# A gated spectral and feed-forward mix: first block loaded in halves, last gated part moved, last store in halves

## The chip, the cores and the metric

The kernel runs on one core of one Trainium2 chip. The metric is device time in microseconds (us): the median of three runs before the change is 1020.85 us (1020.79 to 1021.39). The engines are TensorE (PE, with its weight loads as PEld), VectorE (DVE), ScalarE (ACT), GpSimd (POOL) and SyncE (SP); SP, ACT and POOL each have a queue on which they issue DMAs.

## The reference

```python
x = A_x                                        # 1 x 2048 x 640, fp32
g = sigmoid((x * gate_w).sum(-1))
a = x @ dft_hid_re.T ;  b = x @ dft_hid_im.T
fnet = dft_seq_re @ a - dft_seq_im @ b         # 2048 x 2048 by 2048 x 640
ffn = (gelu(x @ w_gate) * (x @ w_up)) @ w_down # hidden size 1728
return g * fnet + (1 - g) * ffn
```

All in fp32. The kernel gets that precision by splitting an operand into a high part (a copy rounded to the fp32r type) and a low part (the rest), and forms each product from three fp32r matmuls: high by high, high by low, low by high.

## The kernel before, in words

Everything is tiled to 128 partitions, and the 2048 rows of x lie in four column blocks of 512, taken as two pairs. The program has stages: the hidden layer of the feed-forward part (first its plain 128 columns and a mixed remainder, then the rest in a scheme of sums that saves products), the product with w_down, the sequence transform (which makes u), and the last product of u with the hidden-size transform, whose results are multiplied by the gate and added to what already lies in the output.

**The start.** Inside `in_order(ACT, DVE, PE, SP)`, which fixes the order on each engine to that of the code, line 1072 issues the first weights on ACT's queue and line 1073 the first block of x, 128 partitions by 512 columns, on SP's; then SP issues four more weight pieces and four more x pieces. `first_parts` (line 1052) makes the parts of a piece: ACT the high part of x (line 1055), DVE the first weights' high part (line 1057), then DVE the low part of x (line 1060) and of the weights (line 1061). `first_block` (line 379) runs on TensorE, for each of the five pieces, three matmuls high by high (line 387) into three accumulators (pm, pg, pu), three with the low part of x (line 389) and three with the low weights (line 391). Seven matmuls on zeros stand ahead of it.

**The end.** The last of four groups in the u stage needs five parts of u, numbered 15 to 19 in the tile names. TensorE runs `tail` over them for X, Z and V (lines 1552 and 1563), for L (lines 1570, 1571, one accumulator of 512 columns and one of 256), and last 30 matmuls of 256 columns into `last` (yLast, line 1578), which work on gated parts of u. `gated_u` (line 1332) makes one: two products with the gate on DVE (ug, line 1337), the high part on ACT and the low part on DVE (both ue, line 1339). Its calls stand between the sums of Z and V (line 1564), the last one behind them (line 1568). Each sum of Z or V is a DVE instruction that adds the accumulator (line 1566), then `give` (line 1460): a product with the gate on DVE and a store of 256 KB on POOL's queue that adds to the output. ACT and DVE are in the order of the code here too. The end of the program is three plain stores: the first L block by POOL, the second by SP (line 1575), and the 256 columns of `last`, copied by DVE and stored by SP (lines 1580, 1581).

Names: x011h and x011l are the high and low part of the first x pieces, w0h and w0l of the weights, xr and w0r the raw loads; yx and ys are the results of V and Z, yl those of L and `last`.

Of the kernel before, what the change touches and what calls it, by code (L numbers as in the profile page):

```python
# [8 lines left out]
F32 = mybir.dt.float32  # L9
F32R = mybir.dt.float32r  # L10
BF16 = mybir.dt.bfloat16
AF = mybir.ActivationFunctionType
ALU = mybir.AluOpType

P = 128
S, D, F = 2048, 640, 1728
T = 512
NT = S // T
ND = D // P
# [11 lines left out]
def kernel(  # L31
# [27 lines left out]
    nc = tc.nc  # L59
# [11 lines left out]
    def mtile(dt, name):  # L71
        return pool.tile([P, T], dt, tag="m", name=name, bufs=12)
# [4 lines left out]
    def high(hi, raw):  # L77
        nc.scalar.activation(hi, raw, AF.Copy)  # L78
# [300 lines left out]
    def first_block(W, B, tp, t, parts, then):  # L379

        ps = [bank(f"p{n}{tp}{t}") for n in "mgu"]
        ws = [W[n] for n in "mgu"]
        for d in range(ND):
            rh, rl = xpart(B, d, t)
            parts(d)
            for p, w in zip(ps, ws):
                nc.tensor.matmul(p, w[d][0], rh, start=d == 0, stop=False, skip_group_check=True)
            for p, w in zip(ps, ws):
                nc.tensor.matmul(p, w[d][0], rl, start=False, stop=False, skip_group_check=True)
            for p, w in zip(ps, ws):  # L390
                nc.tensor.matmul(p, w[d][1], rh, start=False, stop=d == ND - 1, skip_group_check=True)
        pm, pg, pu = ps
        then()
        mixed_out(pm, tp, t)
        ge = mtile(F32, f"ge{tp}{t}")
        nc.scalar.activation(ge, pg, AF.Gelu_apprx_tanh)
        tt(ge, ge, pu, op=ALU.mult)
        keep(h0[tp], t - 1, ge)
# [643 lines left out]
    B, tiles, load, piece, tsum, his, lows = load_x(0)  # L1042

    def load_piece(d, t):
        raw, src, _ = piece(d, t)
        nc.sync.dma_start(raw, src)
# [5 lines left out]
    def first_parts(d):  # L1052
        raw, _, (xh, xl) = piece(d, 1)
        wh, wl, wr = parts0(d)
        high(xh, raw)
        if d == 0:
            nc.vector.tensor_copy(wh, wr)
        else:
            high(wh, wr)
        low(xh, xl, raw)  # L1060
        low(wh, wl, wr)
# [8 lines left out]
    with in_order(ACT, DVE, PE, mybir.EngineType.SP):  # L1070
        tiles(1)
        load0(nc.scalar, 0)
        load_piece(0, 1)
        for d in range(1, ND):
            load0(nc.sync, d)
            load_piece(d, 1)
        tiles(2)
        load(2)
        pw = bank("pwarm")
        for _ in range(7):  # L1080
            nc.tensor.matmul(pw, warm[:, :P], warm, start=True, stop=True, skip_group_check=True)
        first_block(W0, B, 0, 1, first_parts, second_parts)
        B0, (tsum0, his0, lows0) = B, (tsum, his, lows)
        Bs.append(B)
        B, tiles, load, piece, tsum, his, lows = load_x(1)
        tiles(1)
        load(1)
        tiles(2)
        load(2)
        mixed(Wm, B0, 0, 2)  # L1090
        his((1, 1), (2, 1))
        lows((1, 1), (2, 1))
        split_piece(4, 1)
        plain_gate_up(W0, B0, 0, 2)
        tsum0(1)
        tsum0(3)
        mixed(Wm, B, 1, 1)
        his((1, 2), (2, 2))
        his0("T1", "T3")
        lows((1, 2), (2, 2))  # L1100
        split_piece(4, 2)
        lows0("T1")
        tsum0(2)
        lows0("T3")
        his0("T2")
        tsum0(4)
        plain_gate_up(W0, B, 1, 1)
        his0("T4")
        lows0("T2", "T4")
        W = load_w(1)  # L1110
        nc.sync.dma_start(gwb, gw.to_broadcast([P, D]))
        tsum(1)
        tsum(3)
        mixed(Wm, B, 1, 2)
        his("T1", "T3")
        lows("T1")
        tsum(2)
        lows("T3")
        his("T2")
        tsum(4)  # L1120
        his("T4")
        lows("T2", "T4")
        plain_gate_up(W0, B, 1, 2)
# [50 lines left out]
    p, f = 1, 3  # L1174
# [112 lines left out]
    H = T // 2  # L1287
# [44 lines left out]
    def gated_u(i):  # L1332

        r = ugs[i]
        v = slot(F32, [P, 2, H], f"ug{i}")
        for q in range(2):
            tt(v[:, q], r[q][:, 1, H:], gw[1][:, 1, H:], op=ALU.mult)
        e = slot(F32R, [P, 2, 2, H], f"ue{i}")
        split(e[:, 0], e[:, 1], v)
        ugs[i] = [(e[:, 0, q], e[:, 1, q]) for q in range(2)]  # L1340
# [128 lines left out]
    for i, (tp, b, p) in enumerate(useq[: 3 * ND]):  # L1469
# [22 lines left out]
        if not b:  # L1492
            for q in range(2):
                sv["c11", q] = copy(X[q], f"ys{n}{q}")
            for q in range(2):
                c = sv["c11", q]
# [64 lines left out]
    for k, (ps, w, b, t) in enumerate(((Z, "S4", 3, 1), (V, "A12", 2, 0))):  # L1561
        for q in range(2):
            tail(ps[q], (w, q, True), b)
            gated_u(3 * ND + 2 * k + q)
            v = es[q][t]
            tt(v, v, ps[q], op=ALU.add)
            give(1, 2 * q, t, v)
    gated_u(3 * ND + 4)
    for t, cols, ps in ((0, slice(0, T), L[0]), (1, slice(0, H), L[1][:, :H])):
        tail(ps, ("e5", 0, True), t, cols)  # L1570
        tail(ps, ("e5", 1, False), 2 + t, cols)
# [4 lines left out]
    for q in range(2):  # L1576
        for p in range(ND):
            mm3(last, ukw[0, p]["e5"][q], ugs[3 * ND + p][q], False, p == ND - 1)
    v = mtile(F32, "yl2")[:, :H]
    nc.vector.tensor_copy(v, last)  # L1580
    nc.sync.dma_start(out[3, 4, :, H:], v)
    order.close()


# [62 lines left out]
```

## Time and profile before

| | us |
|---|---|
| median of 3 runs | 1020.85 |
| profiled execution, its own time | 1020.78 |
| its span | 1019.0 |
| TensorE busy | 1013.6 (99%) |
| VectorE busy | 811.6 (80%) |
| ScalarE busy | 494.9 (49%) |
| GpSimd busy | 145.5 (14%) |

The span runs from the first to the last thing the profiler saw; 1.78 us of the execution's own time lie outside it. Times in rows count from the span's start. A matmul's busy time overlaps the next one's, since matmuls are pipelined: the start-to-start distance tells the pace.

### The profile page before, as it was taken

What the parts mean: (1) busy time and instruction counts of PE and PEld (TensorE: products, weight loads), DVE (VectorE), ACT (ScalarE), POOL (GpSimd) and SP (SyncE); (2) the same over time, 40 slices, a digit from 0 to 9 for tenths busy, and PEclk for the clock granted to TensorE, in tenths of its full rate; (3) what the DMA queues carried; (4) which work ended last, traced back from release to release, by engine and by line L of the source; (5) the groups of instructions that cost most, each with busy time, mean ns of one, the idle gap of its engine ahead of it and who ended that gap; (6) DMA issues with size and microseconds to landing.
All of it is one profiled execution on the core that took longest, in us unless ns stands there. A gap on an engine that the chain in (4) does not pass through costs nothing.

```text
span 1019.0 us, 13152 instructions
## 1 busy us (share of the span) xinstructions
PE 1013.6 (99%) x4488; PEld 835.3 (82%) x4488; DVE 811.6 (80%) x1148; ACT 494.9 (49%) x660; POOL 145.5 (14%) x259
## 2 busy tenths in 40 slices
PE   9999999999999999999999999999999999999998
PEld 7888888888888888887888888888888888888887
DVE  6988887978778939967898976878687769797777
ACT  5455455545365637456455443434443345455431
POOL 0113130212123100100010022002100200021013
PEclk9999999999999999999999999999999999999999
DMA  8358797959699978877866579657965878697748
GB/s 283 138 189 300 267 331 235 350 198 351 208 344 365 359 257 275 294 245 259 294 222 219 198 265 333 237 199 264 336 210 195 303 245 289 249 388 219 258 97 132
DMA packets 87795, 265.01 MB, mean 260 GB/s; under 512 B 11216, under 2 KB 19440, under 8 KB 87728
## 3 DMA queue, kind: packets, MB, share of 16 engines
q1 hardware_dynamic: 65392, 194.47, 56.0%
q0 software_dynamic: 22192, 69.50, 20.1%
q8 instruction: 35, 0.57, 0.2%
q14 instruction: 32, 0.26, 0.1%
q10 hardware_dynamic: 144, 0.20, 0.1%
HBM read 194.38 MB, written 69.75 MB: 259 GB/s over the span
## 4 chain that ended last, share of the span: by engine, by line
PE 87%; issue 8%; DVE 2%; POOL 1%; DMA 1%; ACT 1%; POOLq 0%; ACTq 0%; DVEq 0%
PE pX L89 4%; PE pX L90 4%; PE pX L91 4%; PE pL L89 3%; PE pL L90 3%; PE pL L91 3%; PE px L89 3%; PE px L91 3%; PE px L90 3%; PE pZ L89 2%; PE pZ L90 2%; PE pZ L91 2%; PE pV L89 2%; PE pV L90 2%; PE pV L91 2%
## 5 line engine op out<-in xcount | busy, mean ns | idle before, releaser
L78 ACT ACTIVATE ch<-csa 128x1024 fp32r<-128x1024 f32 x32 | 34.0, 1063 | 75.2 <-DVE csa L868 66.9
L81 DVE TENSOR_TENSOR cl<-cra,ch 128x1024 fp32r<-128x1024 f32 x32 | 39.2, 1224 | 28.8 <-ACT ch L78 23.4
L78 ACT ACTIVATE ch<-cra 128x1024 fp32r<-128x1024 f32 x32 | 33.9, 1060 | 57.0 <-PE pY L90 19.2
L81 DVE TENSOR_TENSOR cl<-crb,ch 128x1024 fp32r<-128x1024 f32 x32 | 39.1, 1223 | 13.5 <-ACT ch L78 11.4
L90 PE MATMUL pL<-cl,xah 128*128 128x512 f32 x128 | 49.8, 389 | 0.0
L91 PE MATMUL pL<-ch,xal 128*128 128x512 f32 x128 | 49.8, 389 | 0.0
L89 PE MATMUL pL<-ch,xah 128*128 128x512 f32 x128 | 49.3, 389 | 0.0
L78 ACT ACTIVATE ch<-crb 128x1024 fp32r<-128x1024 f32 x32 | 33.8, 1057 | 22.6 <-DVE cl L81 7.8
L81 DVE TENSOR_TENSOR cl<-csb,ch 128x1024 fp32r<-128x1024 f32 x32 | 39.2, 1225 | 2.0 <-ACT ch L78 0.5
L81 DVE TENSOR_TENSOR cl<-csa,ch 128x1024 fp32r<-128x1024 f32 x32 | 39.1, 1221 | 1.7 <-PE pL L90 0.7
L78 ACT ACTIVATE ch<-csb 128x1024 fp32r<-128x1024 f32 x32 | 34.0, 1064 | 10.3 <-DVE csb L871 6.4
L350 POOL DMA_DIRECT2D hA<-s x48 | 26.2, 546 | 83.1 <-DVE s L708 52.2
L707 ACT ACTIVATE s<-s 128x512 f32<-128x512 f32 x20 | 12.7, 633 | 49.1 <-DVE s L548 33.0
L81 DVE TENSOR_TENSOR kl<-kw,kh 128x1024 fp32r<-128x1024 f32 (+1 forms) x26 | 31.5, 1211 | 3.6 <-ACT kh L78 3.6
L78 ACT ACTIVATE kh<-kw 128x1024 fp32r<-128x1024 f32 (+1 forms) x26 | 27.2, 1046 | 7.9 <-DVE kw L926 4.7
L981 POOL DMA_DIRECT2D out<-ks x12 | 6.5, 543 | 167.1 <-DVE ks L980 166.5
L548 DVE TENSOR_TENSOR s<-s,px 128x512 f32<-128x512 f32 x12 | 8.2, 686 | 27.5 <-ACT s L630 25.9
L1343 POOL DMA_DIRECT2D uA<-c x8 | 4.3, 543 | 170.9 <-DVE c L1430 170.7
L350 POOL DMA_DIRECT2D hT<-s x48 | 26.0, 543 | 17.9 <-DMA hA<-s 3.1
L91 PEld LDWEIGHTS pL<-ch,xal 128*128 128x128 f32 x128 | 24.0, 188 | 5.0
L89 PEld LDWEIGHTS pL<-ch,xah 128*128 128x128 f32 x128 | 24.0, 188 | 5.0
L90 PEld LDWEIGHTS pL<-cl,xah 128*128 128x128 f32 x128 | 24.0, 188 | 5.0
(3089 smaller groups left out, 3471.4 us busy)
## 6 DMA issues: line engine op xcount, KB each, us to landing
cra<-in_ct SPq DMA_DIRECT2D x64, 512.0 KB, 4.0
crb<-in_ct SPq DMA_DIRECT2D x64, 512.0 KB, 4.8
xx<-xtd SPq DMA_DIRECT2D x42, 512.0 KB, 6.1
hA<-s POOLq DMA_DIRECT2D x48, 256.0 KB, 5.9
hT<-s POOLq DMA_DIRECT2D x48, 256.0 KB, 6.4
kr<-hA SPq DMA_DIRECT2D x24, 512.0 KB, 7.9
kr<-hT SPq DMA_DIRECT2D x24, 512.0 KB, 6.3
ux<-uA SPq DMA_DIRECT2D x24, 512.0 KB, 6.0
```

Source lines behind the costliest of these rows:

```text
L78: nc.scalar.activation(hi, raw, AF.Copy)
L81: nc.vector.tensor_tensor(lo, raw, hi.bitcast(F32), op=ALU.subtract)
L89: nc.tensor.matmul(ps, lh, rh, start=first, stop=False, skip_group_check=True)
L90: nc.tensor.matmul(ps, lh, rl, start=False, stop=False, skip_group_check=True)
L91: nc.tensor.matmul(ps, ll, rh, start=False, stop=last, skip_group_check=True)
L350: nc.gpsimd.dma_start(to[:, i], src)
L548: tt(a, a, c, op=ALU.add)
L707: nc.scalar.activation(s2, s2, AF.Gelu_apprx_tanh)
L981: nc.gpsimd.dma_start(out[2 * tp + t, e], src)
L1343: nc.gpsimd.dma_start(to[:, i], src)
```

## The change

Three places are edited. The first x block is loaded as two column halves, the left on SP's queue and the right on ACT's behind the weights; its high part is made in two halves and the first three matmuls become six of 256 columns. The last gated part (19) is made between the sums of the two V halves instead of behind both. The last copy and store is cut in two: 128 columns by DVE and SP, 128 by ACT and its queue.

```diff
@@ first_block
-            for p, w in zip(ps, ws):
-                nc.tensor.matmul(p, w[d][0], rh, start=d == 0, stop=False, skip_group_check=True)
+            for c in (slice(0, T // 2), slice(T // 2, T)) if d == 0 else (slice(0, T),):
+                for p, w in zip(ps, ws):
+                    nc.tensor.matmul(p[:, c], w[d][0], rh[:, c], start=d == 0 and c.start == 0, stop=False, skip_group_check=True)
@@ first_parts
-        high(xh, raw)
         if d == 0:
+            for c in (slice(0, T // 2), slice(T // 2, T)):
+                high(xh[:, c], raw[:, c])
             nc.vector.tensor_copy(wh, wr)
         else:
+            high(xh, raw)
             high(wh, wr)
@@ loads
         load0(nc.scalar, 0)
-        load_piece(0, 1)
+        raw, src, _ = piece(0, 1)
+        for queue, c in ((nc.sync, slice(0, T // 2)), (nc.scalar, slice(T // 2, T))):
+            queue.dma_start(raw[:, c], src[:, c])
@@ the end
             tail(ps[q], (w, q, True), b)
             gated_u(3 * ND + 2 * k + q)
+            if k and not q:
+                gated_u(3 * ND + 4)
             v = es[q][t]
             tt(v, v, ps[q], op=ALU.add)
             give(1, 2 * q, t, v)
-    gated_u(3 * ND + 4)
...
-    v = mtile(F32, "yl2")[:, :H]
-    nc.vector.tensor_copy(v, last)
-    nc.sync.dma_start(out[3, 4, :, H:], v)
+    for name, c in (("yl2", slice(0, P)), ("yl3", slice(P, H))):
+        v = mtile(F32, name)[:, c]
+        if c.start:
+            nc.scalar.activation(v, last[:, c], AF.Copy)
+        else:
+            nc.vector.tensor_copy(v, last[:, c])
+        (nc.scalar if c.start else nc.sync).dma_start(out[3, 4, :, H + c.start : H + c.stop], v)
```

The order of instructions at the places that the prediction speaks of. A semaphore in brackets is one that the instruction waits for: DMAHW of a DMA issued by SP or ACT, DMASW of one issued by POOL.

ACT at the start of the program, before (w0r and xr are the raw weights and x):

```order
L200 DMA w0r0_141<-in_w0 128x384
L78 ACT_TABLE_LOAD
L78 ACTIVATE x011h_151<-xr011_150 128x512 [waits DMAHW1_49]
L78 ACTIVATE x011h_151<-xr011_150 128x512 [waits DMAHW3_49]
L78 ACTIVATE w0h0_144<-w0r0_141 128x384 [waits DMAHW2_49]
```

ACT at the same place, after:

```order
L200 DMA w0r0_141<-in_w0 128x384
L1078 DMA xr011_150<-in_xt 128x256
L78 ACT_TABLE_LOAD
L78 ACTIVATE x011h_151<-xr011_150 128x256 [waits DMAHW1_49]
L78 ACTIVATE x011h_151<-xr011_150 128x256 [waits DMAHW3_49]
L78 ACTIVATE x011h_151<-xr011_150 128x512 [waits DMAHW4_49]
L78 ACTIVATE w0h0_144<-w0r0_141 128x384 [waits DMAHW2_49]
```

ACT issues a second DMA behind the weights, and the first high part is two instructions, each with a wait of its own.

DVE near the end, before: the gated parts 17, 18 and 19 (ug, ue), the V sums (yx0, yx1) and the first L sum:

```order
L81 TENSOR_TENSOR ue17_8590<-ug17_8587,ue17_8590 128x512
L1566 TENSOR_TENSOR yx0_8489<-yx0_8489,yVlast0_8470 128x512
L1461 TENSOR_TENSOR yx0_8489<-yx0_8489,gw1_7708 128x512
L1337 TENSOR_TENSOR ug18_8611<-ux180_8315,gw1_7708 128x256
L1337 TENSOR_TENSOR ug18_8611<-ux181_8316,gw1_7708 128x256
L81 TENSOR_TENSOR ue18_8614<-ug18_8611,ue18_8614 128x512
L1566 TENSOR_TENSOR yx1_8513<-yx1_8513,yVlast1_8471 128x512
L1461 TENSOR_TENSOR yx1_8513<-yx1_8513,gw1_7708 128x512
L1337 TENSOR_TENSOR ug19_8620<-ux190_8359,gw1_7708 128x256
L1337 TENSOR_TENSOR ug19_8620<-ux191_8360,gw1_7708 128x256
L81 TENSOR_TENSOR ue19_8623<-ug19_8620,ue19_8623 128x512
L1573 TENSOR_TENSOR yl0_8656<-yLlast0_8472,gw1_7708 128x512
```

DVE at the same place, after:

```order
L81 TENSOR_TENSOR ue17_8595<-ug17_8592,ue17_8595 128x512
L1342 TENSOR_TENSOR ug19_8598<-ux190_8364,gw1_7713 128x256
L1342 TENSOR_TENSOR ug19_8598<-ux191_8365,gw1_7713 128x256
L81 TENSOR_TENSOR ue19_8601<-ug19_8598,ue19_8601 128x512
L1573 TENSOR_TENSOR yx0_8494<-yx0_8494,yVlast0_8475 128x512
L1466 TENSOR_TENSOR yx0_8494<-yx0_8494,gw1_7713 128x512
L1342 TENSOR_TENSOR ug18_8622<-ux180_8320,gw1_7713 128x256
L1342 TENSOR_TENSOR ug18_8622<-ux181_8321,gw1_7713 128x256
L81 TENSOR_TENSOR ue18_8625<-ug18_8622,ue18_8625 128x512
L1573 TENSOR_TENSOR yx1_8518<-yx1_8518,yVlast1_8476 128x512
L1466 TENSOR_TENSOR yx1_8518<-yx1_8518,gw1_7713 128x512
L1579 TENSOR_TENSOR yl0_8661<-yLlast0_8477,gw1_7713 128x512
```

Part 19 stands ahead of both V sums now, part 18 between them as before, and the second V sum right ahead of L.

ACT at the very end, after (before, nothing followed the last ue):

```order
L78 ACTIVATE ue17_8595<-ug17_8592 128x512 [waits DVE_49,Activation_49]
L78 ACTIVATE ue19_8601<-ug19_8598 128x512 [waits DVE_49,Activation_49]
L78 ACTIVATE ue18_8625<-ug18_8622 128x512 [waits DVE_49]
L1588 ACTIVATE yl3_8732<-yLast_8527 128x128 [waits DMASW3_49,DMASW1_49,DVE_49]
L1591 DMA out_0<-yl3_8732 128x128 [waits Activation_49]
```

ACT's copy of the last 128 columns and its store are new.

## Rows read from the trace of the kernel before

**Rows 1.** Waits of TensorE: line, releaser: total us, times, longest.

```profile
...
PE pm L387 <- ACT x011h L78: 0.5, 1, 0.5
PE yLast L90 <- DVE ue L81: 0.3, 1, 0.3
```

**Rows 2.** Timeline of the start: start, length (us), engine, line, op, tiles [idle before].

```profile
...
0.74 0.41 ACTq L200 DMA_DIRECT2D w0r<-in_w  x1
...
4.12 0.63 ACT L78 ACTIVATE x011h<-xr 128x512 fp32r<-128x512 f32 x1 [1.66 <-DMA xr<-in_xt]
...
4.33 0.36 DVE L1057 CAST w0h<-w0r 128x384 fp32r<-128x384 f32 x1 [3.19 <-DMA w0r<-in_w]
...
4.83 0.63 PE L387 MATMUL pm<-x011h,w0h 128*128 128x512 f32 x1 [0.47 <-ACT x011h L78]
...
5.76 0.39 PE L389 MATMUL pm<-x011l,w0h 128*128 128x512 f32 x1
...
```

**Rows 3.** Timeline of the last 15 us, the same columns.

```profile
...
1005.80 0.69 DVE L81 TENSOR_TENSOR ue<-ug,ue 128x512 fp32r<-128x512 f32 x1 [0.76 <-ACT ue L78]
...
1006.41 0.68 DVE L1566 TENSOR_TENSOR yx<-yx,yVlast 128x512 f32<-128x512 f32 x1
...
1007.13 0.69 DVE L1461 TENSOR_TENSOR yx<-yx,gw 128x512 f32<-128x512 f32 x1
...
1007.74 0.75 DVE L1337 TENSOR_TENSOR ug<-ux,gw 128x256 f32<-128x256 f32 x2
...
1008.59 0.63 ACT L78 ACTIVATE ue<-ug 128x512 fp32r<-128x512 f32 x1 [2.81 <-DVE ug L1337]
...
1009.25 0.69 DVE L81 TENSOR_TENSOR ue<-ug,ue 128x512 fp32r<-128x512 f32 x1 [0.76 <-ACT ue L78]
...
1011.01 0.28 PE L89 MATMUL yLast<-ue,uw00h 128*128 128x256 f32 x1
...
1011.67 0.88 POOL L1462 DMA_DIRECT2D out<-yx  x1 [2.58 <-DVE yx L1461]
...
1012.33 0.28 PE L91 MATMUL yLast<-ue,uw03l 128*128 128x256 f32 x1
...
1013.24 0.68 DVE L1573 TENSOR_TENSOR yl<-yLlast,gw 128x512 f32<-128x512 f32 x1
...
1015.02 0.43 DVE L1574 TENSOR_TENSOR yl<-yl,av 128x256 f32<-128x256 f32 x1
...
1015.71 0.42 DVE L1580 COPY yl<-yLast 128x256 f32<-128x256 f32 x1 [0.26 <-PE yLast L91]
1016.16 0.34 SPq L1581 DMA_DIRECT2D out<-yl  x1
```

**Rows 4.** Stretches: us, busy by engine, granted clock, DMA share, GB/s.

```profile
...
1.75:3.00 1.25, 1.25 (x5) 0.42 (x3) 0.00 (x0) 0.71 (x1) 0.00 (x0) 1.00 0.74 213
3.00:4.70 1.70, 1.36 (x4) 0.18 (x2) 0.36 (x1) 0.58 (x1) 0.00 (x0) 1.00 1.05 391
1013.00:1014.80 1.80, 1.46 (x13) 1.42 (x13) 1.76 (x4) 0.00 (x0) 0.00 (x0) 1.00 1.00 145
1016.10:1017.70 1.60, 0.00 (x0) 0.00 (x0) 0.03 (x1) 0.00 (x0) 0.00 (x0) 1.00 0.93 327
...
```

**Rows 5.** DMA queues from 940 to 955 us: packets, MB, share.

```profile
...
q0 software_dynamic: 197, 0.35, 12.8%
...
```

**Rows 6.** DMA queues from 0 to 3 us (q1 SP, q10 ACT).

```profile
...
q1 hardware_dynamic: 85, 0.17, 18.2%
q10 hardware_dynamic: 60, 0.09, 12.6%
...
```

**Rows 7.** DMA, all queues from 0 to 4.7 us.

```profile
...
DMA packets 579, 0.93 MB, mean 198 GB/s; under 512 B 56, under 2 KB 329, under 8 KB 579
...
```

**Rows 8.** DMA queues from 0 to 3.8 us.

```profile
...
q10 hardware_dynamic: 144, 0.20, 17.5%
...
```

**Rows 9.** Groups by form on ACT: line, op, shapes, count | busy, mean ns | idle.

```profile
...
L78 ACT ACTIVATE xbh<-xm 128x256 fp32r<-128x256 f32 x8 | 3.2, 402 | 0.0
...
```

## Prediction

> **What bounds the kernel now.** I read the waits of TensorE first. In the whole program it waits for another engine at two places that the change touches: 0.5 us before its first real matmul, for the first block of x, and 0.3 us near the end, for the low part of the last gated block [rows 1]. Between them it runs without a break, so what these edges gain or lose is not taken up by anything in the middle: it arrives at the end as it is. Nothing in the kernel leaves room for more than about a microsecond either way, against a time of 1020.78 us for the profiled execution (span 1019.0 and 1.78 us around it); the median of the runs is 0.07 us above it. What a measurement of this kernel can tell from no change is about 0.2%, 2.04 us.
>
> Second, the timeline of the start [rows 2]. The first weights are issued on ScalarE's queue at 0.74 us, the first x block on SP's beside them; ScalarE starts on the block at 4.12, VectorE on the weights at 4.33. The two paths end almost together: the weights' cast at 4.33 + 0.36 = 4.69, the x block's high part at 4.12 + 0.63 = 4.75, the matmul at 4.83. So the x path alone has 0.06 us to give before the weights bound.
>
> Third, the timeline of the last 15 us [rows 3], fourth what the DMA engines do there [rows 4, 5]. The page's shares by engine are no help: both edges are latencies.
>
> **Edit 1, the first x block in halves.** It adds one DMA, one activation and three matmuls, and takes away the wait for the whole block. ScalarE's queue now issues the weights and behind them the second half. By 3.0 us the trace has 85 packets of SP's queue against 60 of ScalarE's [rows 6], SP having started earlier: while both hold work they take turns, packet by packet. A DMA here is 144 packets (128 rows and 16 small ones), a half block too. So the weights are through when about 288 packets have moved and the second half when 576 have (the first half and the second weights on SP's queue, the weights and the second half on ScalarE's). Bounds: if packets set the pace, the 576th goes at 4.7 us, where the trace counts 579 [rows 7]; if bytes do, those four transfers are 656 KB and that is reached near 4.0 (0.17 + 0.09 MB by 3.0 and 0.39 MB per us after [rows 4, 6]). Landing followed the last packet by 0.6 us: the weights' 144th packet was moved by 3.8 [rows 8] and VectorE began at 4.33 [rows 2]. Until 3 us the pace is low (213 GB/s, against 391 later [rows 4]) and looks set by packets; so I take about 4.25 for the last packet of the second half and 4.85 for its landing, later than the whole block before, and 4.05 for the weights.
>
> Then: cast done 4.43, first halves' matmuls from 4.5; second activation 4.87 to 5.28 (0.40 for 256 columns [rows 9]); the low part, one instruction over all 512 columns as before, 5.32 to 6.01; its matmuls at 6.07 where they stood at 5.76 [rows 2]. Cost 0.3 us. The ends: landing with the old block at 4.09 gives 5.31, a gain of 0.45; landing at 5.3 gives a loss of 0.75. The later x pieces are not late for it: the DMA engines are full from 3 us on [rows 4], and SP's fourth piece, which now waits for the weights' landing where the eighth transfer did, goes to a queue that is not empty by then.
>
> The Trainium skill, "DMA: Bandwidth & Descriptors", section "Issuing engines are not separate DMA queues", says that transfers started by different engines run on the same 16 DMA engines and interleave, and that starting them from several only saves issue time. The packet counts agree [rows 6]. By that rule the second queue saves issuing time and brings no bandwidth; the sum above already goes by the counts.
>
> **Edit 2, the last gated part one sum sooner.** On VectorE the step of part 19 (two products, ScalarE's high part, the low part) goes ahead of the two instructions that finish the first V sum. TensorE's 30 last matmuls start 0.12 us apart (1011.01 to 1012.33 is eleven steps [rows 3]); without the stall the eighteen behind 1012.33 end at 1014.49 + 0.28 = 1014.77 instead of 1015.68, just before the copy at 1015.71. So the stall is worth 0.91 us on TensorE.
>
> VectorE after the change, from the low part of 17 at 1005.80, with the intervals of [rows 3] (0.61 from a low part to what follows, 0.85 from the products to ScalarE's start, 0.66 from there to the low part, 0.72 and 0.61 through a sum): products of 19 at 1006.41, low part 1007.92; V sum 8.53, its gate 9.25; products of 18 at 9.86, low part 1011.37; second V sum 11.98, gate 12.70; first L product 1013.31. That was 1013.24 [rows 3]: the same instructions on VectorE, 0.07 later because the low part of 19 no longer stands right before the L sums and a gate does. Part 18's low part, with 0.69 us for it, is ready near 1012.1, just when its matmul asks for it; if that costs 0.1 us, TensorE has it to spare.
>
> What is late next: VectorE ends its L sums at 1015.02 + 0.43 + 0.07 = 1015.52, and the last copy is queued behind them. It starts near 1015.45 instead of 1015.71; the 0.91 us has become 0.26.
>
> The price stands on GpSimd's queue. The two gates of the V sums move 0.61 + 0.85 + 0.66 = 2.12 us later, and each is followed by an accumulating store of 256 KB. The last of these is issued at 1011.67 and its data moves from 1013.0 to 1014.8 with the DMA engines full and only 145 GB/s [rows 3, 4]; then they are idle until the three plain stores (0.52 MB) fill them from 1016.1 to 1017.7 [rows 4]. After the change it is issued at 1013.79 and its data starts near 1015.1, so it runs into the plain stores. If the work adds up, 1015.1 + 1.8 + 1.5 (0.93 of 1.6) = 1018.4 where the data ended at 1017.7: 0.7 later. If the accumulating store only waits and lets others pass, nothing. Nearest row: in a stretch of loads 0.35 MB of such packets held 12.8% of 15 us [rows 5], 1.9 us, which is some 1.4 us for one store. So it adds nearly its full price; I take 0.6.
>
> **Edit 3, the last copy in halves.** The copy of 128 columns on VectorE is taken as 0.28 us, between nothing and the 0.42 of 256 columns [rows 3]: 1015.45 to 1015.73. ScalarE's half waits, by the order's row, for VectorE and not for TensorE: what it needs of VectorE is the other half's copy, which reads the same accumulator. So it runs 1015.78 to 1016.08, and its store is issued at 1016.12, where the one store was issued at 1016.16 [rows 3]. Gain 0.04 at most, and none while the DMA engines are still busy with what is ahead. Rows of half the length could cost up to 0.1 us of transfer; I take 0.
>
> The Trainium skill, "PSUM — Partial Sum Buffer", section "Terms", says that two engines on one bank and quadrant at once are a collision, reads against reads included. The order's row agrees: the copies follow each other. Were they side by side, ScalarE's store would be issued near 1015.2.
>
> **Sum:** +0.3 (start) + 0.6 (stores) + 0 (copy) on 1020.78: 1021.7 us. Ends: -0.45 and -0.05 give 1020.3; +0.75, +0.7 and +0.1 give 1022.3.
>
> **Rivals.**
> 1. *The start gains and the stores hide.* The halves land by bytes, with ScalarE's half no later than the old block, and the accumulating store lets the plain ones through: -0.45 and 0, 1020.3 us. For it: bytes do set the pace from 3 us on [rows 4]; against it: packets taking turns, and ScalarE's half queued behind 192 KB.
> 2. *It does all it says:* the stall's 0.91 us and the start's 0.45 both arrive at the end, 1019.4 us. Against it: the copy behind VectorE's L sums, and three stores that cannot all move faster than 1.5 us.
> 3. *TensorE's clock drops.* The granted clock is 1.00, 2.4 GHz, through the pause of 0.5 us before the first matmul [rows 1, 4]. The change puts a second pause of some 0.3 to 0.8 us between halves. If the clock then fell to 1.2 GHz, each microsecond at that level would lose half a microsecond; from 2.3 us at the lower level (1.15 lost, on 1021.7) the time passes 1022.9 and is slower. With 4 us: 1023.7. For it only that the pause grows; against it that the pause of today left no mark.
>
> **Chances.** Forecast (start and stores both cost something) 62%; rival 1, 27%; rival 2, 6%; rival 3, 3%; 2% for what I don't see. The first three all lie within 2.04 us of before. Faster by over 0.2% would need more than the stall and the start together: 2%. Slower by over 0.2%: rival 3 and a little, 4%. Same: 94%. The range 1020.2 to 1022.4 takes in forecast and rival 1; between 1020.8 and 1022.4 lies the forecast's own.
>
> **What would show it.** Start: ScalarE's second half activation begins near 4.9 (right) or by 4.2 (rival 1); the first low-part matmuls near 6.1. End: no wait of TensorE above 0.1 us in the last matmuls; VectorE's copy starting about 0.6 us after TensorE is done; ScalarE's copy starting as VectorE's ends; the last accumulating store issued near 1013.8 on the old clock, and no idle DMA between it and the plain stores, whose data ends 0.6 later. The forecast is wrong if the second half lands before 4.4, or if the last data ends no later than before counted from TensorE's L sums.

## The result, and the profile after

The changed kernel takes 1023.02 us (median of 14 runs, 1022.76 to 1023.37) against 1020.83 us before (14 runs beside them): ratio 1.002, with a 95% interval of 1.0012 to 1.0028. It is 2.2 us slower. 1021.7 was forecast, with 1022.4 as the upper end. Two of the 14 runs before lie above 1022; the section on the start below takes such runs up. The profiled execution took 1023.00 us, its span 1021.2; before it was 1020.78 and 1019.0, so the 2.2 us lie inside the span.

TensorE's waits after the change:

```profile
...
PE pm L388 <- DVE w0h L1059: 0.2, 1, 0.2
```

The wait for the last gated part [rows 1] is gone, as meant, and so is the half microsecond before the first matmul: what waits for the weights now is 0.2 us. The start in the timeline:

```profile
...
3.82 0.42 ACT L78 ACTIVATE x011h<-xr 128x256 fp32r<-128x256 f32 x1 [0.87 <-DMA xr<-in_xt]
...
4.01 0.36 DVE L1059 CAST w0h<-w0r 128x384 fp32r<-128x384 f32 x1 [2.87 <-DMA w0r<-in_w]
...
4.51 0.55 PE L388 MATMUL pm<-x011h,w0h 128*128 128x256 f32 x1 [0.15 <-DVE w0h L1059]
...
4.87 0.42 ACT L78 ACTIVATE x011h<-xr 128x256 fp32r<-128x256 f32 x1 [0.64 <-DMA xr<-in_xt]
...
6.07 0.50 PE L390 MATMUL pm<-x011l,w0h 128*128 128x512 f32 x1
...
7.57 0.39 PE L388 MATMUL pm<-x011h,w0h 128*128 128x512 f32 x1
...
```

The first half is there at 3.82, 0.3 us before the whole block [rows 2], but the second at 4.87, and the low part, which wants both, lets TensorE begin on it at 6.07 instead of 5.76. At the second piece of x (line 388 again) TensorE is 0.42 us behind (7.15 before), and it stays there: its first yLast matmul is 0.40 later than in [rows 3], VectorE's low part of part 17 0.45 later. The last 15 us:

```profile
...
1006.25 0.69 DVE L81 TENSOR_TENSOR ue<-ug,ue 128x512 fp32r<-128x512 f32 x1 [0.76 <-ACT ue L78]
...
1011.41 0.28 PE L89 MATMUL yLast<-ue,uw00h 128*128 128x256 f32 x1
...
1014.18 0.88 POOL L1467 DMA_DIRECT2D out<-yx  x1 [2.52 <-DVE yx L1466]
...
1014.88 0.28 PE L91 MATMUL yLast<-ue,uw04l 128*128 128x256 f32 x1
...
1015.47 0.58 POOL L1581 DMA_DIRECT2D out<-yl  x1 [0.40 <-DVE yl L1579]
...
1015.82 0.28 DVE L1590 COPY yl<-yLast 128x128 f32<-128x128 f32 x1
1015.92 0.34 SPq L1581 DMA_DIRECT2D out<-yl  x1
1016.13 0.28 ACT L1588 ACTIVATE yl<-yLast 128x128 f32<-128x128 f32 x1 [4.40 <-DVE yl L1590]
1016.36 0.42 SPq L1591 DMA_DIRECT2D out<-yl  x1
1016.44 0.36 ACTq L1591 DMA_DIRECT2D out<-yl  x1
```

Without the start's 0.40 (TensorE) and 0.45 us (the rest) the steps stand where the prediction's chain put them: TensorE's last matmul begins at 1014.48 (1015.39 in the kernel before), the copy at 1015.37 (forecast 1015.45), behind VectorE's L sums; ScalarE's copy begins as VectorE's ends; the last accumulating store is issued at 1013.73 (forecast 1013.79). SP's last store is issued at 1015.91 by that clock, where it was 1016.16. The loss comes behind it. Stretches of that end, with the DMA engines' share and GB/s last:

```profile
...
1014.90:1015.50 0.60, 0.26 (x3) 0.05 (x1) 0.57 (x3) 0.00 (x0) 0.20 (x2) 1.00 0.00 0
1015.50:1017.75 2.25, 0.00 (x0) 0.00 (x0) 0.60 (x2) 0.28 (x1) 0.54 (x1) 1.00 0.96 118
1017.75:1019.35 1.60, 0.00 (x0) 0.00 (x0) 0.00 (x0) 0.00 (x0) 0.00 (x0) 0.88 0.95 324
...
```

The DMA engines are idle until the accumulating store starts (its first packet moves at 1015.63). It then has all 16 engines to itself until 1017.75 (the stretch of 2.25 us, 118 GB/s); the plain stores follow it and take 1.6 us as before. DMA queues while it moves, and in the quarter microsecond behind it (packets, MB, share; q0 GpSimd, q1 SP):

```profile
...
q0 software_dynamic: 142, 0.27, 96.4%
...
```

```profile
...
q0 software_dynamic: 26, 0.09, 100.0%
q1 hardware_dynamic: 8, 0.01, 9.3%
...
```

SP's store of 128 KB was issued at 1015.92. In the kernel before, the same store's first packet moved at 1016.85, 1.37 us after its issue; here it moved at 1017.91, 1.99 us after, when the accumulating store was through. From there on packets of the three queues are mixed. The last landings (KB, us from issue), after and then before:

```profile
...
out<-yl SPq DMA_DIRECT2D x1, 64.0 KB, 3.5
```

```profile
...
out<-yl SPq DMA_DIRECT2D x1, 128.0 KB, 1.9
```

1016.36 + 3.5 = 1019.86 is the last landing, where it was 1016.16 + 1.9 = 1018.06. And from there to the end of the span it takes 1.34 us, where it took 0.94. These views show landings and spans to 0.1 us; the trace's own records give 1019.89 and 1018.11, and 1.33 and 0.90 us behind them.

So the 2.2 us are: 0.45 at the start, 1.35 from VectorE's low part of 17 to the last landing (13.61 us against 12.26; 13.64 and 12.31 by the trace's records), and 0.40 behind that landing.

### The profile page after: what moved, and what is told of

It is laid out like the page before. It is cut to its first block, busy times and chain, and to the rows that moved or that the text cites. A ratio compares the mean times of both kernels' runs of the same rounds, so it can differ in the third digit from the quotient of the medians.

```text
span 1021.2 us, 13163 instructions
## 1 busy us (share of the span) xinstructions
PE 1013.7 (99%) x4491; PEld 835.6 (82%) x4491; DVE 810.9 (79%) x1148; ACT 495.3 (49%) x662; POOL 145.5 (14%) x259
## 4 chain that ended last, share of the span: by engine, by line
PE 87%; issue 8%; DVE 2%; POOL 1%; DMA 1%; ACT 1%; DVEq 0%; ACTq 0%; POOLq 0%
PE pX L89 4%; PE pX L91 4%; PE pX L90 4%; PE pL L89 3%; PE pL L91 3%; PE pL L90 3%; PE px L89 3%; PE px L90 3%; PE px L91 3%; PE pZ L91 2%; PE pZ L89 2%; PE pZ L90 2%; PE pV L89 2%; PE pV L91 2%; PE pV L90 2%
```

## Experiments

Medians of 11 runs each, with the kernel before run beside them on the same chip (its medians there 1020.69 to 1020.87). Differences are against that median, where nothing else is said.

### The three edits alone

Edit 1 alone:

> The kernel before with edit 1 alone (the first x block in two halves on two queues). In the changed kernel the first low-part matmuls began 0.31 us later than before and all of TensorE's later work 0.40 to 0.42 later. Theory A (the halves cost the start, and nothing takes it up again): +0.4 us, 1021.2 us, and TensorE's first yLast matmul 0.4 us later than before. Rival B (the start only moves the beginning; the later loss is all the tail's): within 0.1 us of before, 1020.8. Rival C (something in the start also delays the tail, through later stores): +1 us or more.

Measured: 1021.63 us (1021.36 to 1021.98), +0.93. In its profile TensorE's first yLast matmul came 0.29 later than before and VectorE's low part of 17 only 0.17; from there to the last landing 12.26 us, as before; from the landing to the end 1.37. The median lies between theory A (+0.4) and rival C (+1 or more), and the loss doesn't come as theory A said: 0.17 by the start and 0.43 by the end of the span make up the 0.58 of the profiled execution, which is the fastest of the eleven. The others lie up to 0.6 above it, and no profile shows what they lose.

Edit 2 alone:

> The kernel before with edit 2 alone (the last gated part one sum sooner). Theory A (the last accumulating store, issued 2.1 us later, holds up the plain stores behind it, on whatever queue they are): +1.4 to +1.8 us, about 1022.4; no wait of TensorE for the last part, the last accumulating store's data until about 1017.3 and the plain stores' data only behind it. Rival B (the split of the last store makes the loss, edit 2 itself gives what TensorE gains): 0.26 us faster, 1020.5. Rival C (the accumulating store costs only its own 0.6 us as forecast): 1021.4.

Measured: 1022.21 us (1021.66 to 1023.62), +1.51: theory A. The profiled execution was the longest of the eleven, 1023.62, and shows two things. The tail, stretches as above:

```profile
...
1016.70:1018.95 2.25, 0.14 (x2) 0.00 (x0) 0.78 (x3) 0.00 (x0) 0.58 (x1) 1.00 0.98 116
1018.95:1020.50 1.55, 0.00 (x0) 0.00 (x0) 0.00 (x0) 0.00 (x0) 0.00 (x0) 0.85 0.93 335
...
```

The same 2.25 us for the accumulating store, then the plain stores. From the low part of 17 to the last landing it is 13.41 us, 1.15 more than before, without any of edits 1 and 3. And the start:

```profile
...
4.94 0.77 PE L387 MATMUL pm<-x011h,w0h 128*128 128x512 f32 x1 [0.57 <-ACT x011h L78]
5.50 0.63 PE L387 MATMUL pg<-x011h,w0h 128*128 128x512 f32 x1
...
9.34 0.56 PE L387 MATMUL pg<-x011h,w0h 128*128 128x512 f32 x1
9.74 0.40 PE L387 MATMUL pu<-x011h,w0h 128*128 128x512 f32 x1
...
```

The matmuls of 512 columns start 0.43 us apart until 9.34, and 0.23 from 9.74 on: 1.2 columns per ns, what 1.2 GHz would give, then 2.2. The granted clock is shown as 1.00 in this whole stretch, but the trace's first record of it begins at 9.68 us, just where the pace changes: where there is no record, the view shows 1.00 all the same. TensorE is 2.07 us late at its first yLast matmul, and that is none of edit 2, whose start is the one of before.

Edit 3 alone:

> The kernel before with edit 3 alone (the last copy and store in two halves on two engines). Theory A (the copies follow each other and the split store costs nothing): within 0.2 us of before, 1020.8; ScalarE's copy begins as VectorE's ends. Rival B (rows of half the length and one more queue at the end make the later landing): +0.6 to +1.5 us, 1021.4 to 1022.3.

Measured: 1021.52 us (1020.87 to 1023.35), +0.82. By its profile neither theory: the low part of 17 to the last landing takes 12.34 us, 0.08 more than before (theory A's part holds, and ScalarE's copy began as VectorE's ended); but again 1.35 us from the landing to the end, and a start at half pace until about 7 us.

The three losses add up to 3.3 us and not to 2.2. The 0.4 at the end of the span is in edits 1 and 3 and is there only once in the change, and edits 2 and 3 alone keep the start of before and its scatter (below).

### The accumulating store

In the changed kernel the store of the second V sum is left out:

```diff
...
-            give(1, 2 * q, t, v)
+            if k and q:
+                tt(v, v, gw[1][:, t], op=ALU.mult)
+            else:
+                give(1, 2 * q, t, v)
...
```

> The changed kernel, without its last accumulating store (the sum and the gate of the second V half stay, the store of that block is left out, so one block of the output lacks its last term). Theory A (that store holds up the plain ones): the plain stores' data starts within 1 us of their issue, the last of them about 1.3 to 1.8 us earlier than in the changed kernel, 1021.4 us. Rival B (the split store or the start make the loss): 1022.6 or more.

Measured: 1021.67 us (1021.49 to 1021.93), 1.35 less than the changed kernel (1.2 less, when each is taken against the kernel before beside it): theory A.

```profile
...
1016.30:1018.05 1.75, 0.00 (x0) 0.00 (x0) 0.00 (x0) 0.00 (x0) 0.00 (x0) 1.00 0.90 299
...
```

The plain stores' first packet moves at 1016.39, 1.14 us after the first of them is issued (1015.25), and their data ends at 1018.08. The same omission in the kernel before:

> The kernel before, without its last accumulating store (the sum and the gate stay, so one block of the output lacks its last term); the control to the same omission in the changed kernel, which was worth 1.35 us there. Theory A (the store is hidden before, since its data has ended at 1014.8 and the plain stores' begins at 1016.1): within 0.3 us of before. Rival B (the store costs its time wherever it stands): 1.3 us faster, 1019.5.

Measured: 1021.05 us (1020.14 to 1023.10) against 1020.80 beside it, ratio 1.000 (0.9991 to 1.0009): theory A. The store is free where the DMA engines are idle behind it and costs 1.35 us where the plain stores stand behind it. Is that its size, or the addition? In the changed kernel again, the same block as a store that doesn't add:

```diff
...
-            give(1, 2 * q, t, v)
+            if k and q:
+                tt(v, v, gw[1][:, t], op=ALU.mult)
+                nc.gpsimd.dma_start(out[2 + t, 2 * q], v)
+            else:
+                give(1, 2 * q, t, v)
...
```

> The changed kernel with its last accumulating store made a plain one (same block, size, queue and time of issue; it overwrites the block, so the terms stored there before are lost). Theory A (the price is that of the addition in memory, 145 GB/s against 327 for plain stores): its data moves in 0.8 us instead of 2.25 and is through before the other plain stores come; near the kernel without that store, 1021.7 to 1022.1. Rival B (any 256 KB stored at that place costs the same): 1023.0.

Measured: 1021.71 us (1021.47 to 1022.54): theory A, as if the store weren't there.

```profile
...
1015.10:1015.95 0.85, 0.04 (x1) 0.00 (x0) 0.82 (x3) 0.00 (x0) 0.46 (x1) 1.00 0.80 308
...
```

As a plain store the 256 KB move in 0.85 us at 308 GB/s, on the same queue and at the same place.

How long the accumulating store takes differs from profile to profile. Here it is at its old place, with edit 1 alone and then with one warm-up matmul more (below); as in [rows 4], the stretch holds its 256 KB and nothing else:

```profile
...
1013.25:1015.45 2.20, 1.90 (x16) 1.90 (x17) 2.13 (x5) 0.00 (x0) 0.27 (x1) 1.00 0.85 119
...
```

```profile
...
1013.00:1015.40 2.40, 2.09 (x17) 2.08 (x17) 2.31 (x5) 0.00 (x0) 0.46 (x1) 1.00 0.87 109
...
```

From its first packet to the end of its last it takes 1.95 us in the kernel before and 2.0, 2.1, 2.3, 2.35 and 2.5 in the five other profiles that have it at the old place (edits 1 and 3 alone, and below: both halves on SP's queue, one warm-up matmul more, seven idle loads). In the change it is 2.2. So it isn't longer because it comes later; the kernel before had the shortest of the six.

Nor is it the addition that keeps SP's store back. In four kernels whose last store meets idle DMA engines (the pipelined tails below) its first packet moves 0.84 us after its issue. In nine profiles, that of the kernel before among them, SP's store behind GpSimd's plain one begins 0.15 to 0.2 us before that one's last packet ends, some half a microsecond later than 0.84; in the change, behind the accumulating one, 1.15 us later. Why is open.

### The end of the span

The DMAs of SP and ScalarE take eight semaphores in turn, and a DMA first waits for the one before it with its number. So the order of SP's instructions shows the number of SP's last store, 7 in the kernel before and 0 after (ScalarE's half, one further, has 1):

```
L1581 DMA out<-yl_8724 128x256 [waits DMAHW7_49,DVE_49]
L1591 DMA out<-yl_8729 128x128 [waits DMAHW0_49,DVE_49]
```

SP's last instructions wait for all eight in order of number. With number 7 nothing but the end stands behind the last landing, with number 0 seven more waits do. The trace's records have them: in the changed kernel SP goes on at 1019.91 and through the seven others by 0.06 us each, until 1020.34; in the kernel before the wait that ends at 1018.12 is the last. The next three kernels add loads of 32 bytes that nothing uses, to shift the number.

> Edit 1 alone, and seven loads of 32 bytes on SP's queue before the tail that nothing uses. In the built programs the DMAs of SP and ScalarE take eight semaphores in turn, and SP's last waits go through them from 0 to 7: before, the last store has number 7, with one DMA more it has number 0, and the seven waits behind it come after the landing. From the last landing to the end of the span it was 0.94 and 0.95 us where the last store had number 7 (before, edit 2 alone), and 1.28 to 1.37 where it had 0 or 1 (the other four). Theory A (the place in that list costs 0.4 us): with seven more loads the last store has number 7 again, landing to end 0.95, 1021.2 us, 0.4 less than edit 1 alone. Rival B (that difference comes from something else of edit 1): unchanged, 1021.6.

Measured: 1021.85 us (1021.31 to 1022.64), not faster: theory A's time failed. In its profile the issue of the last store to the end of the span is 2.90 us as against 3.27 with edit 1 alone, which is theory A's number; but TensorE waited 0.5 us for the second weights at the start. The loads may be to blame for that: they stand in the code ahead of the tail, but SP issues the first of them at 0.75 us, ahead of the first x block, and the others at 7.65 to 11.50. And the time around the span is 2.05 us on average of the eleven runs, where it is 1.77 with edit 1 alone. Two kernels that differ in nothing but that number and seven idle loads were to settle it, on the fastest version (below):

> The pipelined tail with eight warm-up matmuls, and one load of 32 bytes on SP's queue before the tail that nothing uses: the last store then has number 0 of the eight semaphores that SP waits for in order at the end, where it had 7. Theory A (the seven waits behind it come after its landing and cost 0.4 us): 1020.4, that is 0.4 above the kernel without the load and above the one with eight loads; last store's issue to the end of the span about 3.0 us where it is 2.6. Rival B (the end's length has to do with edit 1, not with that number): 1020.0, and 2.6 us.

> The same with eight such loads: the last store has number 7 again. Theory A: 1020.0, and 2.6 us from the last store's issue to the end of the span. Rival B: the same time as with one load, whatever it is. Rival C (the loads themselves cost): 1020.4 or more.

Measured: 1020.61 us (1020.19 to 1021.33) with one load, 1020.54 (1019.94 to 1020.80) with eight. The traces agree with theory A in place and size; one load first, then eight (last store's issue, SP's wait for the landing, and TensorE's wait for the second weights):

```profile
...
1016.29 0.34 SPq L1591 DMA_DIRECT2D out<-yl  x1
```

```profile
...
SPq L1652 <- DMA out<-yl: 1.3, 1, 1.3
...
```

```profile
...
PE pm L387 <- ACT w0h L78: 1.1, 1, 1.1
```

```profile
...
1015.83 0.34 SPq L1591 DMA_DIRECT2D out<-yl  x1
```

```profile
...
SPq L1652 <- DMA out<-yl: 0.9, 1, 0.9
...
```

```profile
...
PE pm L387 <- ACT w0h L78: 0.6, 1, 0.6
```

Spans of 1019.3 and 1018.4: 3.01 and 2.57 us from the issue to the end. By the trace's records, all fifteen profiles fall into three groups: from the last landing to the end of the span it is 0.90 or 0.91 us with number 7 (eight of them), 1.33 with number 0 (five) and 1.27 with number 1 (two), one wait of 0.06 us less. In the runs' times the two kernels differ by 0.07 us in the median and 0.28 in the mean, within a scatter of 1.1, so the 0.4 us is shown in the span and not in the time. The eleven spans average 1018.93 and 1018.45 us, 0.48 apart; the time around the span takes 0.2 of that back, 1.77 us with one load and 1.97 with eight (1.84 to 2.10; 1.76 to 1.80 on average in every kernel without loads).

And eight loads cost 0.5 us against none (1020.01, below), as rival C had it. 0.2 of that is the time around the span. The rest can be the start, where the first load is again ahead of the first x block on SP's queue:

```profile
...
0.75 0.35 SPq L1543 DMA_DIRECT2D dum<-in_xz  x1
...
1.15 0.35 SPq L1046 DMA_DIRECT2D xr<-in_xt  x1
...
```

That is from the kernel with one load; without it the first x block is issued at 0.74. With eight loads TensorE's first yLast matmul comes at 1011.59, with eight warm-up matmuls and no load (below) at 1011.22. Both kernels with loads have this start, so it isn't what sets them apart by design; yet their profiles differ in it too, by 0.46 us at that matmul, and only the stretch from the last landing to the end is free of it.

### The start

Edit 1 alone, with both halves on SP's queue and the weights alone on ScalarE's (the line against the changed kernel's):

```diff
-for queue, c in ((nc.sync, slice(0, T // 2)), (nc.scalar, slice(T // 2, T))):
+for queue, c in ((nc.sync, slice(0, T // 2)), (nc.sync, slice(T // 2, T))):
```

> Edit 1 with both halves on SP's queue (the weights alone on ScalarE's, as before). If the packets of the two queues take turns, the first half is through at about 288 packets as in the change, and the second half, on SP's queue right behind it, at about 432 where it was the 576th: landing near 4.4 in place of 4.75 to 4.87. Theory A (the second queue made the halves late): low part of x at 4.9 and its first matmuls at 5.6 or 5.7; TensorE's yLast 0.3 earlier than with edit 1 alone, and with the place of the last store in the waits as there 1021.3. Rival B (the halves as such cost, by one DMA more on SP ahead of the later pieces): as edit 1 alone, 1021.6, or later.

Measured: 1022.05 us (1021.32 to 1022.71), +1.25.

```profile
...
4.63 0.69 DVE L81 TENSOR_TENSOR x011l<-xr,x011h 128x512 fp32r<-128x512 f32 x1 [0.36 <-ACT x011h L78]
...
5.37 0.50 PE L390 MATMUL pm<-x011l,w0h 128*128 128x512 f32 x1
...
7.01 0.63 ACT L78 ACTIVATE x011h<-xr 128x512 fp32r<-128x512 f32 x1 [2.41 <-DMA xr<-in_xt]
...
8.10 0.50 PE L388 MATMUL pm<-x011h,w0h 128*128 128x512 f32 x1 [1.07 <-ACT w0h L78]
...
```

Theory A is right up to 6.6 us: low part at 4.63, its matmuls at 5.37, 0.7 us earlier than in the change. Then rival B: the second piece of x is there at 7.01 (5.51 in the change), and TensorE waits 1.1 us for the second weights, whose high part ScalarE makes behind it. One profile wouldn't show that the one DMA more ahead of it on SP does that, since the second piece comes at 5.37 to 6.49 in profiles with the start of before. But the three kernels with an idle load ahead of it have it at 6.51 to 7.02, and those four alone of the fifteen have a wait for the second weights among TensorE's waits, of 0.5 to 1.1 us. That speaks for the DMA more; with so small a gap between the two groups it isn't shown. On the second queue the second half is late, on the first the pieces behind it; either way the start loses.

One warm-up matmul more, in the kernel before (`range(7)` to `range(8)`):

> The kernel before with eight warm-up matmuls in place of seven, so that TensorE has work until 4.81 us, where its first real matmul began at 4.83. In the profiles of before and of edits 2 and 3 alone TensorE paused there for 0.47, 0.57 and 0.28 us, and its 512-column matmuls then started 0.43 us apart, not 0.23, until 5.3, 9.3 and 6.9 us; of the start in halves, without that pause, all 36 runs lie within 0.7 us, of before 9 of 33 lie 1.5 to 2.4 us above the median. Theory A (the pause is what leaves TensorE at half pace in some runs): no run above 1022, median 1020.4 to 1020.7, the pace of 0.23 reached by 6 us. Rival B (the pause has nothing to do with it): a quarter of the runs stay at 1022.2 to 1023.1. Rival C (the eighth matmul is in the way of the first real one): 0.2 to 0.5 us slower throughout.

Measured: 1020.76 us (1020.18 to 1021.46); before beside it 1020.87 with 5 of 33 runs above 1022. Theory A as far as it goes: no run above 1022, the median 0.06 above its range, and the pace of 0.23 nearly right away in its profile (its first record of the granted clock begins at 4.76 us):

```profile
...
4.78 0.49 PE L387 MATMUL pm<-x011h,w0h 128*128 128x512 f32 x1
5.11 0.40 PE L387 MATMUL pg<-x011h,w0h 128*128 128x512 f32 x1
...
```

The median hardly moves, since the long half pace takes only some runs. By 11 runs alone none above 1022 could be chance, about one time in eight with 22 in 128. Over all runs, 22 of 128 of the kernel before lie above 1022, and of the four other kernels with its start (edits 2 and 3 alone, before without the store, the pipelined tail below) 11 of 44 lie more than 1.5 us above the lowest run of their kernel (25 of the 128 do). Of the ten kernels that begin with halves or with eight warm-up matmuls, no run of 113 lies more than 1.4 us above the lowest of its kernel.

### A better version

The tail again, with the products of the next gated part ahead of the low part of the one before:

```diff
...
+    gv = gated_u(3 * ND)
...
-            gated_u(3 * ND + 2 * k + q)
+            i = 3 * ND + 2 * k + q
+            gn = gated_u(i + 1)
+            gated_split(i, gv)
+            gv = gn
...
-    gated_u(3 * ND + 4)
+    gated_split(3 * ND + 4, gv)
...
```

`gated_u` now makes the two products alone and returns their tile; `gated_split` makes ScalarE's high and VectorE's low part from it.

> The kernel before with the gated steps of the tail in a pipeline: VectorE forms the products of part n+1 while ScalarE makes the high part of part n, so the four idle times of 0.76 us before the low parts go, and nothing is put behind another sum. Theory A (the tail is VectorE's chain, then the accumulating stores): VectorE is about 3 us ahead at the L sums, TensorE's wait for the last part (0.91 us) goes, the last accumulating store is issued some 2 us earlier and its data has ended before the plain stores come: 0.9 to 1.3 us faster, 1019.4 to 1019.8. Rival B (the accumulating stores set the pace from 988 us on, so VectorE's lead only waits in their queue): within 0.3 us of before, 1020.7. Rival C (any new order of the tail costs): 1021.5 or more.

Measured: 1020.06 us (1019.50 to 1021.71), ratio 0.999 (0.9982 to 0.9999): theory A, 0.3 above its range; the profiled execution has half pace until 9.7 us again, and is the slowest by 1.2. With the eighth warm-up matmul:

> The pipelined gated steps of the tail and eight warm-up matmuls together, nothing of the change. In the profile of the pipelined tail TensorE's first yLast matmul to the end of the span took 6.82 us where before took 7.99, though that execution had the start at half pace. Theory A (the two gains are apart from each other): 1.2 us faster than before by the tail and no run with the slow start, 1019.5 to 1019.8, all runs below 1020.6. Rival B (the tail's gain was the luck of the executions): 1020.5 or more.

Measured: 1020.01 us (1019.53 to 1020.55), ratio 0.9989 (0.998 to 0.9998): 0.8 us faster than before and 3.0 than the change, all runs below 1020.6 as theory A had it, its median 0.2 above the range. The profiled execution is the slowest of the eleven, with half pace until 7.2 us, and still ends 0.2 us ahead of before. VectorE's waits in the tail, then the rows of the end:

```profile
...
DVE yl L1587 <- PE yLast L91: 2.7, 1, 2.7
...
```

```profile
...
1009.65 0.88 POOL L1465 DMA_DIRECT2D out<-yx  x1 [0.61 <-DVE yx L1464]
...
1011.92 0.28 PE L89 MATMUL yLast<-ue,uw00h 128*128 128x256 f32 x1
...
1015.40 0.28 PE L91 MATMUL yLast<-ue,uw04l 128*128 128x256 f32 x1
...
1016.17 0.34 SPq L1588 DMA_DIRECT2D out<-yl  x1
```

```profile
...
1013.00:1015.00 2.00, 2.00 (x19) 2.00 (x18) 0.01 (x1) 0.00 (x0) 0.00 (x0) 1.00 0.90 262
1015.00:1016.00 1.00, 0.68 (x6) 0.48 (x4) 0.28 (x1) 0.00 (x0) 0.00 (x0) 1.00 0.00 1
1016.00:1018.00 2.00, 0.00 (x0) 0.00 (x0) 0.14 (x1) 0.00 (x0) 0.00 (x0) 1.00 0.19 66
...
```

In the tail VectorE now waits for TensorE and no longer for ScalarE, and TensorE, once its warm-up has begun, waits for nobody. The last accumulating store is issued 2.0 us earlier than before though the start was 0.9 later; all stores but the last 128 KB are through by 1015.1, the DMA engines idle for the microsecond behind, and the last one lands 1.7 us after its issue.

## Why the prediction was wrong

**The start: right.** The forecast had the second activation at 4.87 and the low-part matmuls at 6.07; both came to the hundredth. So close a hit is luck: in three other profiles with this start the activation begins at 4.73, 4.75 and 4.85. The cost was taken as 0.3 and is 0.40 on TensorE: behind the pause before 6.07 the first matmul took 0.34 to the next instead of 0.23, which was in no row of before. Packets taking turns was the right account of the second half's landing.

**The stall: right.** It went, and what is late next is the copy behind VectorE's L sums. TensorE's last matmul began 0.91 us earlier on the clock of before, the last store was issued 0.25 earlier; both as worked out.

**The copy: right.** ScalarE's half waits for VectorE's; edit 3 costs less than 0.1 us ahead of the last landing.

**The stores: the step that failed.** "If the work adds up, 1015.1 + 1.8 + 1.5 (0.93 of 1.6) = 1018.4 where the data ended at 1017.7: 0.7 later" was the upper end, and 0.6 was taken. The mechanism is the one that the runs show (out with the store, 1.35 us come back; as a plain store, 1.31), the size isn't. On the clock of before (less the 0.45) the store's data ran from 1015.2, the plain stores followed at 1017.30 and took their full 1.6, and the data ended at 1018.9: 1.2 later. Of the 0.6 by which that passes the forecast, 0.3 is the store's length. The others are 0.1 each: the first packet later than 1015.1, 1.6 us for the plain stores and not 1.5, and 0.6 taken where the sum had 0.7.

The 1.8 was one store's. It was read from a stretch that begins ahead of the first packet (1013.12) and ends before the last one is through (1015.07), which is 1.95 us; and the profile of before has the shortest of six at that place, 1.95 to 2.5. It was put down as a fixed price, with a lower one beside it [rows 5] and no allowance above; 0.6, and 0.7 as the end of the range, could only be passed upward. This term is 0.6 of the 1.3 us that the forecast is off.

**The end: not seen.** 0.4 us between the last landing and the end of the span were in no term. Two more DMAs change which semaphore the last store gets, and the traces show seven waits of 0.06 us behind the landing that were ahead of it.

The remainder, 0.3 us, is 0.15 at the start (0.45 where 0.3 was taken) and 0.15 in the last landing, which followed the data by 0.5 instead of 0.35 us.

**The rivals.** Rival 1's two conditions are both refuted: the second half landed late, and the plain stores didn't pass the accumulating one. By the page "DMA: Bandwidth & Descriptors" of the Trainium skill, section "Queues, rings and completion order", an engine goes round between the queues that have work, packet by packet. This trace agrees behind 1017.91 and doesn't before: by the 0.84 us of idle DMA engines SP's store was due near 1016.8, an estimate, and for 1.15 us only GpSimd's packets moved.

Rival 3 rests on a granted clock of 1.00 through the pause [rows 4], and that isn't what the trace says. Its first record of the clock begins at 5.16 us, behind the pause; until then the matmuls of the kernel before, the warm-up ones included, start 0.40 to 0.47 us apart, at half pace. And its sign was wrong: a long half pace is there before the change, in about one run in six by the runs above 1022, and the start in halves, which keeps TensorE at work, has no run that far up. The page "TensorE: Matmul & The Clock Gate" of the Trainium skill, section "Wait — 56ns, not 53.3ns?", gives 427 ns from start to start for 512 columns at 1.2 GHz and 216 at 2.4; the trace has 0.43 and 0.23. What edit 1 takes from the best case it gives back by having no worst one: it is 1.2 us slower by the lowest runs and 1.1 faster by the highest.

## What to carry to other kernels

Ask of a store that is moved later what is queued behind it and what that resource is doing at the new time: a transfer that was free in an idle stretch costs as much of its length as holds up the last ones (here 1.35 of 2.2 us), and an accumulating store takes two to three times as long as a plain one. Read the price of such a transfer from all its rows, not from one: here they lie between 1.95 and 2.5 us. A wait between two engines in a chain was better filled here with the next step's work than shortened by moving one step past another. An idle instruction that is put in for a test has to be looked up in the trace: here it was issued elsewhere than the code has it, and cost time of its own. Where an effect is below a microsecond, read it in the traces from fixed points (one instruction to the last landing, the landing to the end), since runs of one kernel scatter by more.

## What the runs showed of the hardware

- A DMA of 256 KB that adds in memory took 1.95 to 2.5 us from its first packet to its last, in seven profiles in which nothing else moved beside it (six at the old place, and the change); as a plain store it took 0.85 us.
- A store on SP's queue whose first packet came 0.84 us after its issue on idle DMA engines came 1.35 to 1.4 us after it behind a plain store of GpSimd's, and 1.99 behind an accumulating one, each time only when that store was through or nearly so.
- In all fifteen profiles matmuls of 512 columns, the warm-up ones among them, start about 0.43 us apart up to the trace's first record of the granted clock (1.00), and 0.23 behind it (0.33 for the first one behind a pause). That record begins at 3.86 to 5.75 us in the six kernels with the start in halves, whose pause ahead of the first real matmul is at most 0.23 us, and at 5.16, 6.88, 7.21, 9.68 and 9.70 in the five with the start of before and a pause of 0.28 to 0.57. With eight warm-up matmuls it begins at 4.70, 4.76 and 4.81 without a pause and at 7.11 with one of 0.11. So the pause isn't all of it, and what sets the time stays open. For a stretch without a record the view shows 1.00.
- The end of the span is 0.43 us longer when the last DMA has the first of eight semaphore numbers and not the last: seven waits of 0.06 us stand behind its landing.
